# Two reservation rules in a build-time scheduler: large buffers by urgency, buffers for forms of x in order of need

## The chip, the core and the metric

The kernel runs on one core of a Trainium2 chip, float32 throughout. The metric is the device time of one execution in microseconds; the kernel before takes 1688.47 us (median of 4 runs, 1687.31 to 1689.02). The core has five engines with a queue each, which wait for one another by semaphores: TensorE (PE in the profile; its weight loads are PEld), VectorE (DVE), ScalarE (ACT), GpSimd (POOL) and SyncE (SP), which here only issues DMAs.

## The reference

A linear attention without softmax, RMS-normalised, feeds a mixture of four two-layer networks that are all evaluated and weighted:

```
kv  = einsum("bhsd,bhse->bhde", k, v)            # b 8, h 8, s 576, d 64
o   = einsum("bhsd,bhde->bhse", q, kv)
o   = o / sqrt(mean(o*o, -1) + 1e-6) * g_norm
x   = o as (b*s, h*d)                             # 4608 x 512
p   = domain_probs / (sum(domain_probs, -1) + 1e-9)
out = sum over e of p[:, e] * (relu(x @ w1[e]) @ w2[e])   # e 4, w1 512x1024, w2 1024x512
```

## The kernel before, in words

**Tiling.** The 4608 rows are cut into nine chunks of 512: for each of the eight batches its first 512 rows, and one chunk made of the eight remainders of 64 rows. The outer loop runs over the four experts, the inner one over the nine chunks; a pass `s = 9*e + c` is one chunk against one expert. The attention of batch c+1 is worked in among the passes of expert 0, so that x of a chunk is made one pass ahead.

**Fewer products, more sums.** The matrix products of a pass are done by a Strassen-Winograd scheme, for most of them in two levels: seven products of sums and differences of blocks instead of eight. The first pass of all, `up_plain` (line 1050), uses plain products. The others need forms, which are sums of blocks: of w1 and w2 (once for each expert), of x (once for each chunk), of the hidden layer (in each pass). The sums are `combine` (line 375) on VectorE or GpSimd; products go through `halves_of` (line 352; its matmul is L356 in the profile), in `up` (line 946) and in `down` and `down_deep` (1173, 1221).

**Forms of x.** `x_forms(c, key)` (line 854) makes forms 5, 6, 7 and 4 of chunk c, each in a buffer of the kind `xf`; the others lie in the chunk's own halves and in small buffers. After its inner sums each form is copied to DRAM by `keep` (line 894, a DMA of SyncE, L898). Experts 1 to 3 load all seven from there: `x_again` (line 908, issued by `load`, L385), into buffers of the kind `xf` too. There are five of them. Chunk 0 is a special case: pass 0 is plain, so its forms are made for the copies alone.

**Buffers.** The kind `big` is 31 buffers of 128 x 1024 (line 311), later two more. It holds halves of x, weights and their forms, hidden blocks, products and accumulators. A buffer is given to a tile when the operation that first writes it is placed in the order, and returned after its last use.

**The planner.** No order is written by hand. Every operation is entered by `add` (line 59) with a key (its place in the passes: 8.6 is six tenths into pass 8), its engine and a price. `layout` (line 84) plays the program through once, at build time, with these prices, and so fixes the order on each engine and the buffer of each tile; the kernel then issues the operations in that order. For each engine that is free, it looks at the waiting operations within a reach of the first one's key (line 49, `REACH`), and takes:

- for TensorE and SyncE the first that is ready, in the order of keys,
- for the others the ready one with the smallest due time.

A due time is the TensorE work that lies before the operation's key, plus 30 us of allowance if it isn't TensorE's own (`LATE`, line 53), and never later than what its consumers need. `ready` (line 122) decides whether an operation can start: its inputs' writers have been placed, and enough buffers of each kind that it has to open are in the list of free ones (which counts those that will come free at a known time). SyncE's loads must leave some over unless their key is nearly reached:

```python
    SPARE = {"big": 6, "small": 3, "xf": 3}
    FORMS = 9.0
                spare = self.SPARE.get(k, 0) if k != "xf" or op.key < self.FORMS else 0
```

While TensorE has nothing to do before key 0, `layout` fills in transposes into spare banks (`idle`, line 1438, L1440).

**Weights.** Those of expert e+1 come in during the last pass of expert e and the first of the next: `weights_1` and `weights_2` (lines 450, 510), by SyncE into `big`, and for some forms by a ScalarE copy and an accumulating DMA of GpSimd (`subtract_from`, line 436).

Of the kernel before, what the change touches and what calls it, by code (L numbers as in the profile page):

```python
# [35 lines left out]
class Plan:  # L36
# [15 lines left out]
    FORMS = 9.0  # L52
    STEP, LATE = 44.0, 30.0
    SLOW = 6.8

    def __init__(self):
        self.ops = []
# [26 lines left out]
    def layout(self, slots, later, idle, idle_banks, idle_until):  # L84


        free = {k: [(0.0, i) for i in range(len(v))] for k, v in slots.items()}
        slots = {k: list(v) for k, v in slots.items()}
        later = list(later)
        live = {}  # L90
        for b in {b for op in self.ops for b in op.bufs}:
            live[b.kind] = live.get(b.kind, 0) + 1
        ended = {}
        todo = {e: [] for e in self.REACH}
        for n, op in enumerate(self.ops):
            op.n = n
            for e in op.cost:
                todo[e].append(op)
        for e in todo:
            todo[e].sort(key=lambda o: (o.key, o.n))  # L100
        keys, begun, spent = [], [], 0.0
        for op in todo["PE"]:
            keys.append(op.key)
            begun.append(spent)
            spent += op.cost["PE"]
        begun.append(spent)
        for op in self.ops:
            at = begun[bisect.bisect_left(keys, op.key)]
            op.due = at + (0.0 if "PE" in op.cost else self.LATE)
        for op in reversed(self.ops):  # L110
            for d in op.deps:
                cross = self.SAME if op.cost.keys() == d.cost.keys() else self.CROSS
                d.due = min(d.due, op.due - cross - min(d.cost.values()))
        busy = {e: 0.0 for e in todo}
        bus, port = 3.8, 0.0
        lanes = [0.0] * self.LANES
        t = 0.0
        wake = [0.0, 1.6]
        left = len(self.ops)
        order = []  # L120

        def ready(op, eng):
            when = 0.0
            for d in op.deps:
                if d.start is None:
                    return None
            for d in op.deps:
                when = max(when, d.end + (self.SAME if d.eng == eng else self.CROSS))
            need = {}
            for b in op.outs:  # L130
                if b.kind is not None and b.slot is None:
                    need[b.kind] = need.get(b.kind, 0) + 1
            for k, n in need.items():
                spare = self.SPARE.get(k, 0) if k != "xf" or op.key < self.FORMS else 0
                if len(free[k]) < n + (spare if eng == "SP" and op.key > front + 0.1 else 0):
                    return None
                when = max(when, sorted(free[k])[n - 1][0])
            if eng == "SP":
                when = max(when, lanes[0])
            if op.port:  # L140
                when = max(when, port)
            return when

        while left:
            moved = False
            while todo["PE"] and todo["PE"][0].start is not None:
                todo["PE"].pop(0)
            front = todo["PE"][0].key if todo["PE"] else 1e9
            for eng in todo:
                if busy[eng] > t:  # L150
                    continue
                pending = todo[eng]
                while pending and pending[0].start is not None:
                    pending.pop(0)
                if not pending:
                    continue
                reach = pending[0].key + self.REACH[eng]
                best = None
                for op in pending:
                    if op.key > reach:  # L160
                        break
                    if op.start is not None:
                        continue
                    if best is not None and op.due >= best.due:
                        continue
                    when = ready(op, eng)
                    if when is None:
                        continue
                    if when > t:
                        heapq.heappush(wake, when)  # L170
                        continue
                    best = op
                    if eng in ("PE", "SP"):
                        break
                if best is not None:
                    op = best
                    op.start, op.eng = t, eng
                    if eng == "SP":
                        busy[eng] = t + op.cost[eng]
                        bus = max(bus, t + 1.5) + op.kb / 215.0  # L180
                        op.end = bus + 0.5
                        lanes = lanes[1:] + [op.end]
                    else:
                        op.end = busy[eng] = t + op.cost[eng]
                        if op.kb:
                            op.end += 9.0 if op.kb == 512 else 8.0
                    if op.port:
                        port = op.end
                        heapq.heappush(wake, port)
                    for b in op.outs:  # L190
                        if b.kind is not None and b.slot is None:
                            free[b.kind].sort()
                            b.slot = free[b.kind].pop(0)[1]
                            b.ap = slots[b.kind][b.slot]
                    for b in op.bufs:
                        b.left -= 1
                        if b.left == 0 and b.kind is not None:
                            end = max(o.end for o in [op] + b.readers + b.writers) + self.CROSS
                            free[b.kind].append((end, b.slot))
                            live[b.kind] -= 1  # L200
                            ended[b.kind] = max(end, ended.get(b.kind, 0.0))
                            for rule in [r for r in later if not any(live.get(k) for k in r[0])]:
                                later.remove(rule)
                                end = max(ended[k] for k in rule[0])
                                for ap in rule[2]:
                                    free.setdefault(rule[1], []).append((end, len(slots[rule[1]])))
                                    slots[rule[1]].append(ap)
                                heapq.heappush(wake, end)
                    heapq.heappush(wake, busy[eng])
                    heapq.heappush(wake, op.end + self.SAME)  # L210
                    heapq.heappush(wake, op.end + self.CROSS)
                    order.append(op)
                    left -= 1
                    moved = True
                if eng == "PE" and busy[eng] <= t and 1.6 <= t and front < idle_until:
                    kind, spare = next((
                        (k, f) for k in idle_banks for f in free[k] if f[0] <= t
                    ), (None, None))
                    if spare is not None:
                        took = 0.43 if t < self.SLOW else 0.23  # L220
                        op = Op(front, {"PE": took}, None, (), (), 0, False)
                        op.start, op.eng, op.end = t, eng, t + took
                        op.fn = lambda eng, bank=slots[kind][spare[1]]: idle(bank)
                        busy[eng] = op.end
                        free[kind].remove(spare)
                        free[kind].append((op.end, spare[1]))
                        heapq.heappush(wake, op.end)
                        order.append(op)
                        moved = True
            if moved:  # L230
                continue
            while wake and wake[0] <= t:
                heapq.heappop(wake)
            assert wake, ("no operation can start", t, left, {
                e: (todo[e][0].key, todo[e][0].fn) for e in todo if todo[e]
            }, {k: len(v) for k, v in free.items()})
            t = heapq.heappop(wake)
        self.length = max(o.end for o in order)
        return order
# [1251 lines left out]
```

## Time and profile before

| | |
|---|---|
| median of 4 runs | 1688.47 us (1687.31 to 1689.02) |
| the profiled execution, its own time | 1688.64 us |
| its span, first to last instruction | 1686.5 us |
| TensorE matmul busy, and weight loads | 1676.9 us (99%), 1571.7 us (93%) |
| VectorE, ScalarE, GpSimd busy | 1240.4, 978.2, 715.2 us (74%, 58%, 42%) |
| DMA traffic | 234.27 MB, mean 139 GB/s |
| granted TensorE clock | 1.000 |

A line of the profile names a line of the kernel, an engine, an operation, and written tiles before read ones by kind (`xf<-big`); a count after x, then times. `SPq` is SyncE's queue: what it shows is the issue of a DMA. L379 is every sum made by `combine`, so its groups are told apart by tiles. A table of waits gives the sum in us, how often, and the longest. A line of a stretch gives its length, then the busy time of PE, PEld, DVE, ACT and POOL with their instructions, the granted clock, the DMA share and GB/s. The chain of waits is followed back from the last instruction, each step to what released it.

### The profile page before, as it was taken

How to read it: one execution, taken by the hardware profiler on the slowest of the kernel's cores; microseconds unless marked ns; L12 is line 12 of the kernel's file. 1: busy time of each engine (PE TensorE's matmuls, PEld its weight loads, DVE VectorE, ACT ScalarE, POOL GpSimd, SP SyncE). 2: the span in 40 equal slices, each digit the busy share in tenths (PEclk: the TensorE clock that was granted, in tenths of full speed). 3: DMA queues.
4: the chain of work that ended last, by engine and by line, in shares of the span. 5: the costliest groups of instructions: out<-in, count | busy, mean ns of one | idle time of the engine just before them, and what ended most of it. 6: DMA issues, size and time to landing. Idle time of an engine off the chain costs nothing.

```text
span 1686.5 us, 66495 instructions
## 1 busy us (share of the span) xinstructions
PE 1676.9 (99%) x29038; PEld 1571.7 (93%) x29038; DVE 1240.4 (74%) x2045; ACT 978.2 (58%) x2405; POOL 715.2 (42%) x672
## 2 busy tenths in 40 slices
PE   9999999999999999999999999999999999999998
PEld 6687888888889999999999999999999999999996
DVE  4865665575787788777787887877787886877774
ACT  3454555455555666666666666666666666666662
POOL 3613433333454344344455445444446446444431
PEclk9999999999999999999999999999999999999999
DMA  9855453642556344444568444444478444444442
GB/s 240 252 182 157 161 156 105 203 140 96 199 160 163 115 114 114 114 114 110 132 179 200 115 114 114 115 115 113 111 189 201 121 114 115 115 114 114 115 102 51
DMA packets 172330, 234.27 MB, mean 139 GB/s; under 512 B 61576, under 2 KB 112648, under 8 KB 172040
## 3 DMA queue, kind: packets, MB, share of 16 engines
q1 hardware_dynamic: 148968, 193.32, 36.2%
q0 software_dynamic: 23072, 36.71, 14.9%
q8 instruction: 228, 3.74, 0.9%
q14 instruction: 62, 0.51, 0.1%
HBM read 155.79 MB, written 74.19 MB: 136 GB/s over the span
## 4 chain that ended last, share of the span: by engine, by line
PE 99%; DMA 0%; issue 0%; ACT 0%; POOL 0%; DVE 0%; POOLq 0%
PE u L356 47%; PE db L356 32%; PE ab L356 14%; PE ab L716 1%; PE ab L761 1%; PE ab L693 1%; PE ab L743 1%; PE ab L1440 1%; DMA xf<-x 0%; PE ab L805 0%; PE ab L697 0%; PE db L743 0%; PE ab L787 0%; PE ab L821 0%; PE u L743 0%
## 5 line engine op out<-in xcount | busy, mean ns | idle before, releaser
L379 DVE TENSOR_TENSOR big<-big,big 128x1024 f32<-128x1024 f32 (+1 forms) x517 | 501.9, 985 | 43.2 <-ACT big L959 16.7
L356 PE MATMUL u<-xf,big 128*64 128x128 f32 x7072 | 504.8, 273 | 0.8 <-DMA xf<-x 0.8
L356 PEld LDWEIGHTS u<-xf,big 128*64 128x64 f32 x7072 | 409.5, 137 | 5.2 <-DMA xf<-x 1.0
L356 PE MATMUL u<-xf,w1y 128*64 128x128 f32 x5304 | 382.8, 273 | 0.0
L356 PE MATMUL db<-big,big 128*64 128x128 f32 (+1 forms) x4328 | 362.1, 307 | 0.0
L1003 DVE TENSOR_TENSOR big<-u,snap 128x256 f32<-128x256 f32 x464 | 194.5, 422 | 213.3 <-PE u L356 147.4
L356 PEld LDWEIGHTS u<-xf,w1y 128*64 128x64 f32 x5304 | 307.7, 137 | 4.3 <-issue 1.3
L356 PEld LDWEIGHTS db<-big,big 128*64 128x64 f32 x4328 | 264.4, 137 | 39.3 <-issue 0.5
L995 ACT ACTIVATE snap<-u 128x256 f32<-128x256 f32 x490 | 188.0, 384 | 193.7 <-PE u L356 138.7
L379 POOL TENSOR_TENSOR big<-big,big 128x256 f32<-128x256 f32 (+1 forms) x156 | 191.1, 1228 | 167.3 <-DVE big L379 75.0
L995 ACT ACTIVATE big<-u 128x256 f32<-128x256 f32 x464 | 177.6, 385 | 89.2 <-PE u L356 69.0
L379 POOL TENSOR_TENSOR big<-big 128x512 f32<-128x512 f32 (+1 forms) x76 | 95.5, 1257 | 161.1 <-DVE big L379 104.8
L1304 ACT ACTIVATE snap<-db 128x256 f32<-128x256 f32 (+1 forms) x230 | 82.6, 359 | 114.2 <-PE db L356 101.7
L959 ACT ACTIVATE big<-big 128x1024 f32<-128x1024 f32 x133 | 139.9, 1052 | 4.4 <-DVE big L379 4.0
L1312 DVE TENSOR_TENSOR big<-ab,snap 128x256 f32<-128x256 f32 x164 | 69.2, 422 | 58.4 <-PE ab L356 28.5
L1161 POOL DMA_DIRECT2D out_dram<-big x98 | 88.4, 1025 | 55.8 <-ACT big L1138 43.5
L1342 POOL TENSOR_TENSOR big<-big 128x512 f32<-128x512 f32 x34 | 44.1, 1297 | 154.0 <-DVE big L379 140.7
L995 ACT ACTIVATE u<-u 128x256 f32<-128x256 f32 x245 | 91.0, 372 | 28.5 <-PE u L356 14.3
L379 DVE TENSOR_TENSOR big<-big 128x512 f32<-128x512 f32 (+1 forms) x121 | 103.4, 858 | 0.4 <-ACT big L1138 0.2
L356 PE MATMUL ab<-big,big 128*64 128x128 f32 (+1 forms) x1352 | 94.7, 276 | 0.1
L356 PE MATMUL db<-small,big 128*64 128x128 f32 x1240 | 90.6, 273 | 0.0
L356 PE MATMUL ab<-kv,big 128*64 128x128 f32 x1200 | 83.2, 273 | 0.0
(178 smaller groups left out, 2415.4 us busy)
## 6 DMA issues: line engine op xcount, KB each, us to landing
xf<-x SPq DMA_DIRECT2D x108, 512.0 KB, 3.6
out_dram<-big POOLq DMA_DIRECT2D x82, 256.0 KB, 5.6
xf<-x_h SPq DMA_DIRECT2D x81, 256.0 KB, 3.1
xf<-x SPq DMA_DIRECT2D x81, 256.0 KB, 3.7
x<-xf SPq DMA_DIRECT2D x36, 512.0 KB, 4.9
big<-in_moe_w_dram SPq DMA_DIRECT2D x31, 512.0 KB, 5.8
x_h<-big SPq DMA_DIRECT2D x18, 512.0 KB, 3.3
big<-in_moe_w_dram POOLq DMA_DIRECT2D x17, 512.0 KB, 6.2
```

Of the source, the lines that this page charges most:

```text
L356: nc.tensor.matmul(out_[cols], lhsT=lhsT[:, cols], rhs=rhs, **kw)
L379: lambda eng: adder(eng).tensor_tensor(out=out_(), in0=a(), in1=b(), op=op),
L693: nc.tensor.transpose(bank.ap[:, rs], qt.ap[:, rs], ident[:])
L716: nc.tensor.matmul(bank.ap[r * D:(r + 1) * D, o * D:(o + 1) * D], lhsT=ks[r], rhs=vs[r], start=(j == 0), stop=(j == len(sets) - 1), skip_g ...
L743: nc.tensor.matmul(raw[r].ap[c * D:(c + 1) * D, (o * NR + i) * D:(o * NR + i + 1) * D], lhsT=qTs[hp].ap[half, at:at + D], rhs=kv.ap[half, ...
L959: lambda eng: nc.scalar.activation(out=b.ap[:], in_=b.ap[:], func=ACT.Relu),
L995: lambda eng: nc.scalar.activation(out=where(), in_=ps.ap[:, 0:HN], func=ACT.Copy),
L1003: lambda eng: nc.vector.tensor_tensor(out=block(whole, a, t), in0=src.ap[:, 0:HN], in1=add_.ap[:], op=ALU.add),
L1161: nc.gpsimd.dma_start(out=dst, in_=cell(i)[parts, :], accum_op=ALU.add)
L1304: lambda eng: nc.scalar.activation(out=where(), in_=group_of(ps.ap), func=ACT.Copy),
L1312: lambda eng: nc.vector.tensor_tensor(out=cell(tq, dq), in0=group_of(src.ap), in1=group_of(add_.ap), op=ALU.add,),
L1342: lambda eng: adder(eng).tensor_tensor(out=whole(to), in0=whole(a), in1=whole(b), op=ALU.add),
```

## The change

Three constants name the kinds concerned and a tolerance, and two rules are added to `ready`.

**Large buffers.** `waiting["big"]` holds each operation, other than a SyncE load, whose inputs have all been placed and which still has to open a large buffer, with the planned end of its last input. An operation that wants a large buffer may take one only if the free ones exceed its own need by the number of waiting operations that have an earlier due time and whose inputs end within 0.3 us from now. SyncE's loads have no claim of their own, but are held to the rule.

**Forms of x.** `first["xf"]` holds each operation that opens a buffer of the kind `xf` and has not been placed. No operation may open such a buffer while another one there has an earlier due time. This holds for `x_forms` and `x_again` alike.

Prices, due times, keys, numbers of buffers and the operations themselves stay.

```diff
@@ -52,6 +52,7 @@
     FORMS = 9.0
     STEP, LATE = 44.0, 30.0
     SLOW = 6.8
+    SHARED, AHEAD, INORDER = ("big",), 0.3, ("xf",)
@@ -111,6 +112,34 @@
             for d in op.deps:
                 cross = self.SAME if op.cost.keys() == d.cost.keys() else self.CROSS
                 d.due = min(d.due, op.due - cross - min(d.cost.values()))
+        missing, after = {}, {op: [] for op in self.ops}
+        for op in self.ops:
+            missing[op] = len(op.deps)
+            for d in op.deps:
+                after[d].append(op)
+        waiting = {k: {} for k in self.SHARED}
+
+        def arm(op):
+            for b in op.outs:
+                if b.kind in waiting and b.slot is None and "SP" not in op.cost:
+                    waiting[b.kind][op] = max([d.end for d in op.deps] or [0.0])
+
+        for op in self.ops:
+            if not missing[op]:
+                arm(op)
+        first, known = {k: {} for k in self.INORDER}, set()
+        for op in self.ops:
+            for b in op.outs:
+                if b.kind in first and b not in known:
+                    known.add(b)
+                    first[b.kind][op] = True
+
+        def claimed(kind, op):
+            return sum(
+                1 for o, since in waiting[kind].items()
+                if o.due < op.due and since <= t + self.AHEAD and o is not op
+            )
+
@@ -133,6 +162,10 @@
                 if len(free[k]) < n + (spare if eng == "SP" and op.key > front + 0.1 else 0):
                     return None
+                if k in waiting and len(free[k]) < n + claimed(k, op):
+                    return None
+                if k in first and any(o.due < op.due for o in first[k] if o is not op):
+                    return None
                 when = max(when, sorted(free[k])[n - 1][0])
@@ -192,6 +225,12 @@
                             b.slot = free[b.kind].pop(0)[1]
                             b.ap = slots[b.kind][b.slot]
+                    for held in list(waiting.values()) + list(first.values()):
+                        held.pop(op, None)
+                    for o in after[op]:
+                        missing[o] -= 1
+                        if not missing[o]:
+                            arm(o)
                     for b in op.bufs:
```

## The prediction

> **What bounds the kernel now.** I read the page first, then the waits of TensorE, then the record in stretches, and last the places at which the two new rules can act. The page:
>
> ```profile
> span 1686.5 us, 66495 instructions
> PE 1676.9 (99%) x29038; PEld 1571.7 (93%) x29038; DVE 1240.4 (74%) x2045; ACT 978.2 (58%) x2405; POOL 715.2 (42%) x672
> ```
>
> TensorE is busy 99%. The modelled ends of matmuls can flatter that number, so I went to the waits of TensorE, all five of them (sum, times, longest):
>
> ```profile
> PE ab L716 <- issue: 1.9, 1, 1.9
> PE ab L1440 <- POOL ident masks.py:199: 1.4, 1, 1.4
> PE u L356 <- DMA xf<-x: 0.8, 1, 0.8
> PE ab L1440 <- issue: 0.4, 1, 0.4
> PE ab L821 <- ACT big L769: 0.3, 1, 0.3
> ```
>
> They sum to 4.8 us. The timeline puts the three of L716 and L1440, 3.7 us, before 24 us. Only 1.1 us of waiting lies later: 0.3 at 65.64 us (L821) and 0.8 at 536 us, where a form of x comes late. The record in stretches (PE, PEld, DVE, ACT, POOL busy, clock, DMA):
>
> ```profile
> 30.00:40.00 10.00, 10.00 (x100) 4.93 (x98) 7.28 (x17) 3.33 (x9) 0.12 (x1) 1.00 0.94 236
> 40.00:50.00 10.00, 10.00 (x113) 4.39 (x110) 9.85 (x14) 4.75 (x12) 5.52 (x7) 1.00 0.76 174
> 480.00:520.00 40.00, 39.98 (x685) 37.90 (x682) 31.83 (x58) 21.57 (x52) 13.88 (x16) 1.00 0.67 185
> 520.00:560.00 40.00, 39.21 (x720) 38.96 (x718) 33.50 (x64) 24.84 (x60) 17.68 (x17) 1.00 0.56 134
> 560.00:600.00 40.00, 40.00 (x736) 39.82 (x733) 30.79 (x56) 25.34 (x66) 16.22 (x12) 1.00 0.41 121
> 600.00:640.00 40.00, 40.00 (x738) 40.00 (x736) 32.21 (x54) 25.14 (x65) 17.91 (x16) 1.00 0.44 113
> ```
>
> From 600 us on both TensorE columns are full, while VectorE has about 8 of every 40 us free and ScalarE 15. So at a given amount of matmul work the time is this floor plus whatever makes TensorE wait. The change alters no instruction, only their order and their buffers, so it can take away 4.8 us at most by waits, and can add without limit.
>
> **What the Trainium skill says.** Perfetto Trace Analysis, "Identifying the Most-Contended Engine": matmul busy time is a bad metric, and the busy share of weight loads is the good one. The trace agrees: weight loads fill 40.00 of 40 us after 600 us, but only 4.39 of 10 at 40 to 50 us, where the matmuls have 512 columns. The same page, "Optimization Strategy": gaps that repeat on the engine that should be saturated can mean that buffers ran out. No such gap is in TensorE's waits, so a scarce buffer does not stop it now. DMA: Bandwidth & Descriptors, "Anatomy of one DMA — SWDGE (gpsimd) path": DMA engines do not wait on semaphores, the issuing sequencer does. SyncE's own waits agree: a load that waits for a buffer holds all loads behind it.
>
> ```profile
> SPq L385 <- PE u L356: 938.8, 208, 9.0
> ```
>
> **The change, part by part.**
>
> (1) Forms of x are placed by due time. The keys that sort them come from lines of the planner that the change leaves alone; they are keys, not chip times. For forms 5, 6, 4, 7 of chunk 0 they are 71.1, 71.9, 72.6 and 85.6; for chunk 1 they are 59.2, 59.9, 60.7 and 85.8. Chunk 0's forms serve only the copies kept in DRAM, so the rule puts them behind 5, 6 and 4 of chunk 1, and form 7 of chunk 1 behind all four of them. Today three of chunk 0's run early, the first at 39 us; chunk 1's stand at 68.26 (POOL), 72.23, 73.57 and 90.31 us:
>
> ```profile
> 39.05 0.68 DVE L379 TENSOR_TENSOR xf<-big 128x512 f32<-128x512 f32 x1
> 73.57 0.69 DVE L379 TENSOR_TENSOR xf<-big,xf 128x512 f32<-128x512 f32 x1
> 90.31 0.68 DVE L379 TENSOR_TENSOR xf<-big,big 128x512 f32<-128x512 f32 x1
> 103.58 0.61 PE L356 MATMUL u<-xf,big 128*64 128x128 f32 x8
> ```
>
> Each moved form is one operation of 0.68 us, one of 0.42 and two of 0.28: 1.66 us; three make 5.0 us of VectorE work that leaves 39 to 60 us. TensorE waits there for nothing, so I count the relief as 0, with 0.3 (L821) as its best. At the new place VectorE has the room (10.9 of 20 us at 80 to 100).
>
> The five buffers decide what is late next. Chunk 1 holds three until TensorE has read them, so chunk 0's four go through two in two turns. A turn is 1.66 of work, some 0.6 to issue the copy, and 4.9 to land (the page's median for x<-xf): 7.2 us. Form 7 of chunk 1 starts at 74.2 + 2 x 7.2 = 88.6 and is ready at 90.3; TensorE reads it at 103.58. That leaves 13 us of cover, cost 0. Their copies move too: on SyncE, two at 62.79 and one or two later wait for the new work, and the q, k and v loads of chunk 2 and 3 stand behind them. Those loads feed attention a pass later, and SyncE has a gap of 8.6 us there (95.1 to 103.7), so 0. The two large buffers of chunk 0 are given back some 13 to 17 us later; that is part of (3).
>
> (2) The first forms of expert 1. Today's written order loads form 1 of chunk 1 (due 503.6) and form 3 of chunk 0 (494.1) before form 1 of chunk 0 (469.5), because only keys under 9 must leave three buffers. A buffer is thus parked for 60 us, and later loads come when TensorE has no reserve left. The chain at that place:
>
> ```profile
> 528.34 1.33 PE u L356 x24
> 529.67 0.02 issue
> 529.69 6.39 DMA xf<-x
> 536.08 0.04 issue
> 536.12 1.09 PE u L356 x16
> ```
>
> With the rule these two stand behind, all five buffers turn over, and the wait goes: -0.8 us. If another load takes its place, 0.
>
> (3) Large buffers are kept. In the written order of before, 1031 large buffers are given out; in 685 cases three or fewer of the pool were left, so the rule acts everywhere, not at one place. It moves buffers from operations with time to those without. As TensorE waits for no such operation, there is no gain to have. The cost is bounded from below by 0, and from above by loads that come too late: weights. The last quarter of w1 of expert 1 is issued at 467.47 and lands about 5.8 us later. POOL forms two sums at 473.54 and 476.36 (2.4 each), and the inner sums end near 487.3. The x form used with it is issued at 498.33 and lands 3.6 later, at 501.9. So the weights have about 15 us of cover, VectorE its 8 of 40 us. I take 0.
>
> Before 24 us and after the last matmul (1681.8, then 4.7 us of drain) nothing changes: at first at least 15 large buffers are free and no form of x is made; at the end six or more are free.
>
> **Sum.** -0.8 (2), 0 for (1) and (3), -0.1 as a third of the 0.3 at L821. Profiled execution: 1686.5 - 0.9 = 1685.6 span, with the 2.1 around it 1687.7 against its own 1688.64. The median of the runs is 0.17 lower than that execution, so I forecast 1687.6, a change of -0.05%. No difference below 0.2%, 3.4 us, can be told from none.
>
> **The rivals.** *Inert* (0.10): another load is as late, 1688.5. For it: loads of forms wait for TensorE 208 times anyway. *Likeliest* (0.58): 1687.6, own range 1685.3 to 1690.
>
> *Weights too late* (0.20, slower): an operation with an earlier due time claims each buffer that comes free; the loads of the next expert also must leave six, and their due time counts 0.55 us for an issue that needs 5.8 to land. At 15 us of delay the cover is used up; each us beyond stops TensorE at each of three expert changes. From 15 + (3.4 + 0.8) / 3 = 16.4 us it is slower by more than 0.2%. At 18 us it is 9 us: 1696.6; at 20 us 1703. Against it: a load's urgency rises with time, and claims fall away once served.
>
> *Form 7 late* (0.07, slower): if VectorE's queue or SyncE doubles each turn, form 7 comes at 74.2 + 28.8 + 1.7 = 104.7, only 1 us late; only tripled turns, 119.1 us, lose 15 less what TensorE can take in between, about 8: 1695.
>
> *Faster* (0.05): TensorE's small attention pieces cost a pause at each change of shape; its weight loads show some 19 us of such pauses at the attention lines, 0.2 to 0.3 each. If the new order put 14 more of them side by side: 14 x 0.3 = 4.2, 1684.2. Nothing in the rules aims at that.
>
> **How the numbers follow.** Same: 0.58 + 0.10 = 0.68. Slower: 0.20 + 0.07 = 0.27. Faster: 0.05. The low end 1685.2 is the bound of faster; the high end 1697.5 takes in half of the late weights (0.10) and most of form 7 (0.05): 0.83 inside.
>
> **What would show it.** Right: first form of chunk 0 after 70 us instead of 39; loads at 447 to 535 us in order of need; no wait of TensorE for xf at 536; its waits after 25 us at or under 1 us; weight loads later by less than 15 us. Wrong: waits of TensorE for big or xf at 440 to 540, 870 to 930 or 1280 to 1330 us; gaps on TensorE between 60 and 110; or a different TensorE pace with no waits, which would mean that the order of shapes moved the time.

## The result, and the profile after

The changed kernel takes 1686.1 us (median of 42 runs, 1684.49 to 1690.85) against 1688.03 us (63 runs): a ratio of 0.9988, 95% interval 0.9984 to 0.9993. In a second series it was 0.9984 (0.9978 to 0.9991), 1685.96 against 1688.13. So it is faster by 1.9 to 2.2 us, 0.12 to 0.16%. The prediction said 1687.6, within 0.2% of before, with a gain of 0.9 us at the end of its sum.

The page of the changed kernel, its span and busy times:

```profile
span 1684.3 us, 66427 instructions
PE 1675.2 (99%) x29038; PEld 1571.5 (93%) x29038; DVE 1218.0 (72%) x2050; ACT 980.7 (58%) x2405; POOL 703.6 (42%) x667
```

The same 29038 matmuls, 2.2 us less span. Five sums have moved from GpSimd to VectorE (672 to 667, 2045 to 2050): the planner also chooses the engine of a sum. Code lines stand 39 further down in this kernel: L395 is the product that was L356, L424 the load that was L385. All waits of TensorE:

```profile
PE ab L755 <- issue: 1.8, 1, 1.8
PE ab L1479 <- POOL ident masks.py:199: 1.4, 1, 1.4
PE ab L860 <- ACT big L808: 0.3, 1, 0.3
PE ab L1479 <- issue: 0.2, 1, 0.2
PE ab L755 <- DMA big<-in_v_dram: 0.2, 1, 0.2
```

The wait for a form of x is gone; 0.3 us is left after the first 25 us (L860, the old L821). The stretches around the change of expert, in the columns of the prediction:

```profile
480.00:520.00 40.00, 40.00 (x690) 38.20 (x686) 33.33 (x61) 23.83 (x54) 17.97 (x21) 1.00 0.61 176
520.00:560.00 40.00, 40.00 (x738) 40.00 (x734) 32.02 (x59) 24.73 (x61) 18.58 (x17) 1.00 0.61 140
560.00:600.00 40.00, 40.00 (x738) 40.00 (x736) 33.16 (x57) 26.02 (x68) 17.99 (x16) 1.00 0.43 122
```

The count in brackets after TensorE's busy time is the one to read. A stretch full of the short products holds 738 matmuls, 54 ns each. Before, the three held 685, 720 and 736; now 690, 738 and 738. That is 25 matmuls, 1.4 us, though the two busy times of the first stretch differ by only 0.02 us.

Stretches by the clock shift against one another from kernel to kernel, so for the comparison I take the time from the start of one matmul in the trace to that of another, by their place among the 29038 (the count is the same in all kernels):

| stage, by matmul | before | after | difference |
|---|---|---|---|
| start: first to 500th | 42.23 us | 41.90 us | -0.33 |
| attention and expert 0: to the 7001st | 412.59 | 412.17 | -0.42 |
| last pass of expert 0: to the 7501st | 35.72 | 35.82 | +0.10 |
| change to expert 1: to the 9501st | 110.70 | 109.17 | -1.53 |
| experts 1 to 3: to the 28501st | 1037.73 | 1037.68 | -0.05 |
| last product and drain | 46.18 | 46.22 | +0.04 |

The start differs from one execution to the next by more than the whole effect: over the 13 profiles of this study it takes 40.5 to 45.7 us, and 41.9 and 43.0 in the two profiles of the changed kernel, so its -0.33 means nothing. The stages behind it repeat: the second profile of the changed kernel gave 412.17, 35.82, 109.17 and 1037.69 again. The order of before was profiled twice too (the second time as rules_off, below): 412.59 and 412.59, but 110.70 and 110.97 at the change of expert, where its wait for a form of x took 0.8 us once and 1.1 the other time. So a difference of 0.1 us in the attention stage can be read, and at the change of expert the gain is 1.5 to 1.8 us.

### The profile page after: what moved, and what is told of

Read it like the earlier page. It is cut to its first block, busy times and chain, and to the rows that moved or that the text cites. A ratio compares the mean times of both kernels' runs of the same rounds, so it can differ in the third digit from the quotient of the medians.

```text
span 1684.3 us, 66427 instructions
## 1 busy us (share of the span) xinstructions
PE 1675.2 (99%) x29038; PEld 1571.5 (93%) x29038; DVE 1218.0 (72%) x2050; ACT 980.7 (58%) x2405; POOL 703.6 (42%) x667
## 4 chain that ended last, share of the span: by engine, by line
PE 99%; DMA 1%; issue 0%; ACT 0%; SPq 0%; DVE 0%; ACTq 0%
PE u L395 47%; PE db L395 32%; PE ab L395 14%; PE ab L755 1%; PE ab L800 1%; PE ab L732 1%; PE ab L782 1%; DMA big<-in_v_dram 1%; PE ab L844 0%; PE ab L826 0%; PE db L782 0%; PE ab L860 0%; PE ab L1479 0%; SPq L424 0%; PE ab L736 0%
## 5 line engine op out<-in xcount | busy, mean ns | idle before, releaser
L418 DVE TENSOR_TENSOR big<-big,big 128x1024 f32<-128x1024 f32 (+1 forms) x525 | 509.4, 986 | 51.4 <-ACT big L998 21.3
L395 PE MATMUL u<-xf,big 128*64 128x128 f32 x6784 | 486.5, 273 | 0.2
L395 PEld LDWEIGHTS u<-xf,big 128*64 128x64 f32 x6784 | 392.8, 137 | 5.7 <-issue 1.3
L395 PE MATMUL u<-xf,w1y 128*64 128x128 f32 x5304 | 386.7, 273 | 0.0
L1042 DVE TENSOR_TENSOR big<-u,snap 128x256 f32<-128x256 f32 x478 | 200.9, 422 | 250.2 <-PE u L395 153.3
L395 PE MATMUL db<-big,big 128*64 128x128 f32 (+1 forms) x4304 | 362.2, 307 | 0.0
L418 POOL TENSOR_TENSOR big<-big,big 128x256 f32<-128x256 f32 (+1 forms) x204 | 236.2, 1170 | 261.0 <-DVE big L418 124.1
L395 PEld LDWEIGHTS u<-xf,w1y 128*64 128x64 f32 x5304 | 308.9, 137 | 3.0 <-issue 0.5
L395 PEld LDWEIGHTS db<-big,big 128*64 128x64 f32 x4304 | 263.4, 137 | 39.3 <-issue 0.3
L1034 ACT ACTIVATE big<-u 128x256 f32<-128x256 f32 x478 | 182.9, 385 | 80.3 <-PE u L395 57.2
L1343 ACT ACTIVATE snap<-db 128x256 f32<-128x256 f32 (+1 forms) x230 | 82.5, 358 | 110.8 <-PE db L395 103.5
L395 PE MATMUL db<-small,big 128*64 128x128 f32 x1512 | 113.8, 274 | 0.0
L1200 POOL DMA_DIRECT2D out_dram<-big x106 | 94.1, 1028 | 34.5 <-ACT big L1177 29.6
L1381 POOL TENSOR_TENSOR big<-big 128x512 f32<-128x512 f32 x19 | 24.8, 1306 | 166.2 <-DVE big L418 134.2
L395 PE MATMUL ab<-big,big 128*64 128x128 f32 (+1 forms) x1328 | 93.4, 276 | 0.0
L1177 ACT ACTIVATE big<-big,p_all 128x256 f32<-128x256 f32 x186 | 88.2, 501 | 4.1 <-POOL big L1381 3.7
```

Source lines behind the costliest of these rows:

```text
L395: nc.tensor.matmul(out_[cols], lhsT=lhsT[:, cols], rhs=rhs, **kw)
L418: lambda eng: adder(eng).tensor_tensor(out=out_(), in0=a(), in1=b(), op=op),
L1034: lambda eng: nc.scalar.activation(out=where(), in_=ps.ap[:, 0:HN], func=ACT.Copy),
L1042: lambda eng: nc.vector.tensor_tensor(out=block(whole, a, t), in0=src.ap[:, 0:HN], in1=add_.ap[:], op=ALU.add),
L1177: lambda eng: nc.scalar.activation(out=cell(i, half), in_=ap(), func=ACT.Copy, scale=prob()),
L1200: nc.gpsimd.dma_start(out=dst, in_=cell(i)[parts, :], accum_op=ALU.add)
```

## The experiments

Three theories were set against each other. **Expert change:** the gain is the wait at 536 us, and what else stops TensorE between 490 and 600. **Shapes:** the new order has fewer changes between small attention pieces and products on TensorE, each of which costs a pause. **Large buffers:** their rule pays by itself, in expert 0 too. The rule for large buffers with no rule for forms of x has no run: with it the planner comes to a point in pass 8 at which no operation can start, so there is no such order.

### One rule at a time

```diff
# xf_loads: changed kernel, only this part of the rules
-    SHARED, AHEAD, INORDER = ("big",), 0.3, ("xf",)
+    SHARED, AHEAD, INORDER = (), 0.3, ("xf",)
-                if k in first and any(
+                if k in first and eng == "SP" and any(
# xf_sums: the same with   eng != "SP"
# xf_only: the first edit alone
# big_xfloads: the second edit alone
```

> Kernel before, with the in-order rule for forms of x held only against SyncE's loads (experts 1 to 3 and the change to them); the order up to about 430 us is that of before. Parked-buffer theory (the gain is the wait of TensorE for a form of x at 536 us): no wait for xf between 500 and 560, 1.0 to 1.4 us faster than before, half or more of the change's gain. Theory of shapes (the gain comes from fewer pauses at small attention pieces before 420 us): 0, within 0.3 us. Theory of large buffers (their rule makes the gain): 0, within 0.3 us.

> Kernel before, with the in-order rule held only against the sums on VectorE and GpSimd that make forms of x during expert 0. Parked-buffer theory: the wait for a form of x at about 536 us stays, 0.5 to 1.2 us; time as before within 0.5 us. Theory of shapes: up to 0.5 us faster, seen on TensorE between 80 and 420 us. The prediction's part (1): no wait of TensorE added between 60 and 110 us, form 7 of chunk 1 in time.

> Both halves of the in-order rule for forms of x, no rule for large buffers. Parked-buffer theory: as the loads alone, 1.0 to 1.6 us faster than before, no wait for xf at 500 to 560. Theory of large buffers: a third or less of the change's gain of 1.9 us, under 0.7 us.

> The changed kernel without the in-order rule for the sums: large buffers by urgency, and SyncE's loads of forms in order. Parked-buffer theory: 1.0 to 1.6 us faster than before, the same as with the loads alone within 0.5 us. Theory of large buffers: 0.5 us or more faster than the loads alone, with less waiting on TensorE somewhere. Rival of late weights: waits of TensorE for big at 440 to 540, 870 to 930 or 1280 to 1330 us; the prediction expects none.

| kernel | median (before: 1687.98) | ratio, 95% | change to expert 1 | attention stage |
|---|---|---|---|---|
| before | | | 110.70 us (110.97) | 412.59 us |
| xf_loads | 1687.37 | 0.9998 (0.9990 to 1.0006) | 110.03 | 412.59 |
| xf_sums | 1687.89 | 1.0003 (0.9995 to 1.0011) | 110.97 | 411.89 |
| xf_only | 1687.96 | 0.9999 (0.9991 to 1.0007) | 110.31 | 411.89 |
| big_xfloads | 1686.41 | 0.9991 (0.9983 to 1.0000) | 109.17 | 412.77 |

The times cannot tell the first three from before, so the 1.0 us or more that was expected of xf_loads and xf_only did not come. The trace shows how much did at the expert change in the profiled execution: 0.67 and 0.39 us, a few tenths more against the second profile of before. With the loads in order the wait for xf is gone, but another has taken part of its place. TensorE's waits of xf_loads, all but those of the first 25 us:

```profile
PE db L395 <- ACT snap L1343: 0.5, 1, 0.5
PE ab L860 <- ACT big L808: 0.3, 1, 0.3
```

And its three stretches:

```profile
480.00:520.00 40.00, 39.52 (x678) 37.55 (x676) 31.03 (x55) 22.28 (x52) 18.88 (x18) 1.00 0.67 179
520.00:560.00 40.00, 40.00 (x738) 40.00 (x736) 33.94 (x62) 23.35 (x60) 20.25 (x17) 1.00 0.56 136
560.00:600.00 40.00, 40.00 (x734) 39.82 (x732) 29.86 (x55) 25.90 (x67) 17.25 (x14) 1.00 0.38 114
```

The 18 matmuls missing at 520 to 560 are back, while 480 to 520 lacks 12 now, where before lacked 5. The rule for large buffers removes that remainder: 110.03 to 109.17, with the same loads. What is lost here can be read one level below TensorE's own list, in the waits of its weight loads. Between 485 and 600 us, first those of before, then those of xf_loads:

```profile
PEld u L356 <- DMA xf<-x: 1.0, 1, 1.0
PEld db L356 <- ACT ab L1304: 0.3, 1, 0.3
PEld db L356 <- ACT big L1304: 0.2, 1, 0.2
```

```profile
PEld db L395 <- ACT snap L1343: 0.7, 1, 0.7
PEld db L395 <- ACT big L1343: 0.2, 1, 0.2
```

The first list adds up to 1.5 us, which is what the full change gains in this stage; the second to 0.9, which is what the rule for large buffers gains on top of the loads. big_xfloads and the changed kernel have no wait of a weight load in this stretch. All waits but that for xf are for ScalarE (L1304, in the later text L1343), which copies a product out of one of the two `db` banks. In the timeline of before, the weight load of the 0.3 starts at 511.96 us, right after ScalarE's copy of a product that TensorE had only just finished (511.54 to 511.91), with eight matmuls of another product in between; in xf_loads no other product lies between. My reading is that this time is lost where TensorE's order comes back to `db` too soon; the records do not name the bank. How a rule for buffers changes that order was not traced. Nor can it be read from VectorE: before has one wait of 2.3 us there for an output copy that still held a large buffer, but it lasts from 512.6 to 515.0 us, after the 0.3 had passed and 78 us ahead of the 0.2. xf_loads has one as long, over at 513.1 us, a microsecond before its 0.7 begins.

In xf_sums, too, the expected wait for xf did not stay: 1.4 us of waiting for ScalarE's snapshot (L1343) stood in its place, and the stage took 110.97 us. In both kernels whose loads are not held in order, TensorE is stopped there by one thing or another.

big_xfloads against xf_loads is the pair that decides: the theory of the parked buffer alone expected the same time within 0.5 us, that of large buffers a lead of 0.5 or more; the medians differ by 0.96 and the stage by 0.86. The intervals of the two overlap; it is the stage that decides: against 110.03 here, 109.17 came back in six profiles, those of the changed kernel (twice), big_xfloads and, below, big_late, late_02 and pack.

The attention stage has an effect of its own. With the sums held in order it is 0.70 us shorter than before (xf_sums, xf_only), and 0.60 shorter when the rule for large buffers is there too (412.77 to 412.17). The rule for large buffers makes it 0.2 to 0.3 longer. The full change is left with -0.42.

### The rule for large buffers at the expert change only

```diff
# big_late: on top of big_xfloads
-                if k in waiting and len(free[k]) < n + claimed(k, op):
+                if k in waiting and front >= 8.0 and len(free[k]) < n + claimed(k, op):
```

> Kernel before, with SyncE's loads of forms in order and the rule for large buffers only once TensorE's front has reached pass 8 (about 430 us); up to there the order is that of before. Theory of the expert change (both rules pay between 490 and 600 us and nowhere else): TensorE takes 109.2 us there, as with the change, against 110.7 before; 1.2 to 1.9 us faster than before in the span. Theory that the rule for large buffers pays in expert 0 too: 0.5 us or more of the change's gain missing.

1686.15 us against 1688.24, ratio 0.9989 (0.9981 to 0.9997): the time of the full change within the noise. The change of expert takes 109.17 us, the same as with the full change, and the attention stage 412.48, 0.3 more than with it. The stretches:

```profile
480.00:520.00 40.00, 40.00 (x690) 38.27 (x688) 31.28 (x62) 23.69 (x55) 21.20 (x20) 1.00 0.71 185
520.00:560.00 40.00, 40.00 (x737) 40.00 (x735) 31.54 (x62) 23.99 (x62) 16.97 (x18) 1.00 0.55 128
560.00:600.00 40.00, 40.00 (x738) 40.00 (x736) 30.55 (x53) 24.59 (x65) 18.11 (x15) 1.00 0.42 126
```

So the eight passes before it, in which both rules also act with the full change, contribute 0.3 us in the trace, too little for the times to show. The theory of the expert change holds for most of the gain, 1.53 us of about 2. Of these the loads in order give 0.67, and the rule for large buffers on top of them 0.86.

### Later weights

```diff
# late_02: on top of the changed kernel, in ready()
+            if need.get("big") and eng == "SP" and op.kb == 512 and not op.deps and op.key > 7.9:
+                if op.key > front - 0.2:
+                    return None
# late_04: the same with 0.4
```

> The changed kernel; SyncE's loads of the weights of experts 1 to 3 are held until TensorE's front is 0.2 of a pass beyond their key (before and after: from 0.1 ahead of it), so they come roughly 5 to 13 us later. The prediction's cover of 15 us: TensorE loses under 1 us at each expert change, within 0.2% of the changed kernel. Rival of late weights with no cover: 3 to 10 us at each change, 1695 to 1715.

> As the run before, held until 0.4 of a pass beyond the key, roughly 9 us later than there and up to 22 us later than in the changed kernel. Cover of 15 us: about 2 to 7 us lost at each of three changes, 1692 to 1707, seen as waits of TensorE near 500, 930 and 1330 us. If nothing is lost the cover was larger than predicted; if much more, smaller.

late_02: 1687.2 against 1688.24, ratio 0.9993 (0.9985 to 1.0001). In the trace it loses nothing: 109.17 us at the first change, 1037.35 for the passes that follow. That is its fastest execution, 1685.03 us; the median is 1.1 to 1.2 us behind that of the changed kernel, so others may lose a little. late_04: 1700.48 us, ratio 1.0069 (1.0056 to 1.0083). The two longest waits of TensorE (L398 is the product here):

```profile
PE u L398 <- DVE big L1045: 6.1, 2, 3.3
PE u L398 <- ACT snap L1037: 2.5, 2, 1.6
```

The stretches around the second change of expert:

```profile
880.00:920.00 40.00, 39.13 (x718) 38.89 (x716) 32.47 (x56) 26.91 (x64) 21.54 (x23) 1.00 0.79 192
920.00:960.00 40.00, 37.25 (x682) 36.99 (x680) 34.56 (x67) 22.85 (x59) 24.48 (x24) 1.00 0.71 147
```

76 matmuls are missing here, 4.1 us, and TensorE waits again at 1307 and 1323 us, at the third change; at the first it loses 0.16 us in all. Delays against the changed kernel, from the issue of each load in the traces: at the second change, late_02 has at most 14.7 us (w2) and 7.6 (w1) and loses nothing; late_04 has 9.2 to 21.3 us and loses, in the profiled execution, 10.7 us after the 9501st matmul, 5.3 at each of the two changes on average, within the 2 to 7 expected. This execution, 1696.19 us, is the fastest of four; by the median late_04 is 14 us behind the changed kernel, 7 at each of the two changes if it is lost there too. At the first change late_04 delays w2 by 11 to 24 us and the last quarter of w1 by 11.8, at no loss, which was not expected. The rival of late weights exists, then. In the profiled executions its cover at the second and third change ends between 15 and 21 us of delay if w2 sets it, between 8 and 21 if w1 does; the prediction worked out 15, for w1 at the first change, where the 11.8 did no harm. The changed kernel doesn't use it up: its own last quarter of w1 is issued at 464.71 us, 2.8 us earlier than before, and the largest shift that it brings, the third load of w2 at the second and third change, is 10 us (889.49 to 899.85, and 1274.86 to 1285.32).

### Four buffers for forms of x

```diff
-        "big": (31, 2 * NT), "w1y": (7, 768), "xf": (5, 2 * NT), "snap": (5, HN),
+        "big": (31, 2 * NT), "w1y": (7, 768), "xf": (4, 2 * NT), "snap": (5, HN),
```

> The changed kernel with four buffers for forms of x instead of five. The prediction's part (2) held that the wait at 536 us came from one of five buffers being parked for 60 us; this parks one for good, with the order kept. If a missing buffer is what costs: TensorE waits for xf again, 0.5 us or more between 490 and 600, and it may at each of the later passes (24 of them, up to 0.3 us each, 7 us in all). If the order of the loads is what counts: 109.2 us there as with the change, no wait for xf after 600, within 1 us of the changed kernel.

1688.85 against 1688.13, ratio 1.0004 (0.9995 to 1.0013): 2.9 us behind the changed kernel on the same chip. Neither expectation is met. TensorE waits for no form of x, as the order theory says, yet the change of expert takes 110.58 us and the passes after it 1.4 us more than with the change. What it waits for, besides the start and L860:

```profile
PE u L395 <- DVE big L1042: 0.7, 1, 0.7
PE u L395 <- ACT big L1034: 0.5, 1, 0.5
```

Both (at 870 and 587 us) are waits for work on large tiles. So one buffer less for forms of x does cost, 1.4 us at the change of expert, about what the change gains there, but it does not show as a wait for xf: TensorE stops for other tiles. How the shortage gets from one kind to the other was not traced. And a buffer taken away for good is more than one parked for 60 us.

### The rules switched off, and the change again

```diff
# rules_off
-    SHARED, AHEAD, INORDER = ("big",), 0.3, ("xf",)
+    SHARED, AHEAD, INORDER = (), 0.3, ()
```

> The text of the changed kernel with both rules switched off, so that the order and the buffers are those of before instruction by instruction. All theories: the span of before, 1685.8 us in the median, the wait for a form of x at 536 us there, TensorE 110.7 us between 490 and 602. What is open: the changed kernel and every variant of it so far spend 1.8 to 1.9 us around the span, before 2.1. If 1.8 here too, 0.3 us of the measured gain of 1.9 comes with the program's text and not from the rules; if 2.1, with the order.

> The changed kernel unaltered, on the chip of the two runs above, to set them against: 1.6 us less span than before in the median, 1.8 us around the span.

rules_off: 1688.29 against 1688.13, ratio 0.9998 (0.9990 to 1.0006); median span 1686.1 us, as before; the wait for xf is there again, and the change of expert takes 110.97 us, the attention stage 412.59. Its profiled execution is long (1692.36 us) because the first 500 matmuls took 45.7 us:

```profile
PE u L395 <- DMA xf<-x: 1.1, 1, 1.1
```

Around the span it spends 2.11 us, as before (2.10), where the changed kernel spends 1.79. So 0.3 us of the difference lie outside the first and last instruction and come with the order, not with the text. after_again has a median span of 1684.2 us, 1.9 less than before in that series; 1.9 and 0.3 are its 2.2. The stages behind the start, -0.42 and -1.53 with the small ones, add up to 1.9 as well.

### Fewer changes of shape

```diff
# pack: on top of the changed kernel, in TensorE's choice (bookkeeping left out);
# op.small is a piece that is no L356 product
+                    if eng == "PE" and best is not None:
+                        if op.key > best.key + 0.2:
+                            break
+                        if op.small:
+                            best = op
+                            break
+                        continue
+                    if eng == "PE" and op.small and not small and op.key > front + 0.2:
+                        held.append(op)
+                        if len(held) < 2:
+                            continue
+                        best = held[0]
+                        break
                     best = op
-                    if eng in ("PE", "SP"):
+                    if eng == "SP" or (eng == "PE" and (op.small or not small)):
                         break
+                if best is None and held:
+                    best = held[0]
...
                     op.start, op.eng = t, eng
+                    if eng == "PE":
+                        small = op.small
```

> The changed kernel, with one more rule for TensorE: after a small attention piece it takes another one if one is ready within 0.2 of a pass, and a single one far ahead of the front is held until a second is ready. Changes between small pieces and products in TensorE's order fall from 161 to 147 (before: 167). Theory of shapes (each change costs 0.1 to 0.15 us): 1.4 to 2.1 us faster than the changed kernel, between 80 and 420 us. If the pauses do not depend on neighbours: 0.

1684.89 us, ratio to before 0.9980 (0.9972 to 0.9987): ahead of both kernels in the median, by 3.3 and by 1.1 to 1.2 us, though its interval overlaps that of the change, so the second lead is likely and not settled. In the trace the attention stage takes 411.49 us, 0.68 less than with the change, where 1.4 to 2.1 was expected. One wait at 65.7 us is longer; it takes the place of the 0.3 us at L860 (L414 is the product in this kernel):

```profile
PE u L414 <- ACT u L1053: 0.6, 1, 0.6
```

Without the 0.3 us more it would have been 0.9 us for 14 changes of shape: 0.05 to 0.07 us each, where the prediction put 0.3. That supports the theory of shapes as a mechanism, by one order. It does not explain the change itself: before has 167 changes of shape, xf_sums 165, big_xfloads 163 and the changed kernel 161, and their attention stages take 412.59, 411.89, 412.77 and 412.17 us. That the order of the sums moves this stage is measured; how it does so was not found.

## Why the prediction was right

**The class and the floor: right in the main.** Where TensorE is full its pace did not change: experts 1 to 3 past the first change keep theirs within 0.05 us. Faster by 0.12% is within the 0.2% band at 0.68, and the range holds it. Two statements were too strong: that no difference below 0.2% can be told from none (with 42 and 63 runs this one was), and that the floor plus TensorE's list of waits is the whole time.

**Part (2), the forms of expert 1: right that the wait goes, near in its size.** Forecast -0.8 us for loads in order; xf_loads measured -0.67 (110.70 to 110.03; -0.94 against the second profile of before). 0.5 us came back as a wait on ScalarE. That the parked buffer made the wait is not settled: xf_sums does not hold the loads in order, and its wait for xf went too.

**Part (3), large buffers: the step that failed.** It said "As TensorE waits for no such operation, there is no gain to have", after "a scarce buffer does not stop it now". The same loads with and without the rule take 109.17 and 110.03 us: -0.86 where 0 stood. The list of TensorE's waits leaves small pauses out. Its own table of stretches had a sign: at 560 to 600 us TensorE is busy 40.00, but with 736 matmuls and 39.82 us of weight loads, where the full stretch after it has 738 and 40.00. (A low share of weight loads is a sign only between stretches of like shapes: the 4.39 of 10 us at 40 to 50 us goes with 512-column matmuls, and TensorE is busy for all 10 there.) The waits of the weight loads name 0.5 us there besides that for xf. Its other half held: no loss by late weights, and a cover that the delayed loads don't contradict.

**Part (1), the forms of expert 0: no loss, as it said, but by a smaller margin than worked out, and the relief was not 0.** That "TensorE waits there for nothing" hid a gain here too: the sums in order take 0.6 to 0.7 us off the attention stage. The free time of VectorE at the new place is 9.1 us of 20; the 10.9 is what it was busy. Sums and products of this stage in the changed kernel:

```profile
76.31 0.68 DVE L418 TENSOR_TENSOR xf<-big 128x512 f32<-128x512 f32 x1
89.80 0.69 DVE L418 TENSOR_TENSOR xf<-big,xf 128x512 f32<-128x512 f32 x1 [1.64 <-PE u L395]
97.39 0.68 DVE L418 TENSOR_TENSOR xf<-big,big 128x512 f32<-128x512 f32 x1
102.01 0.61 PE L395 MATMUL u<-xf,big 128*64 128x128 f32 x8
```

Chunk 0's forms moved from 39 us to 76, behind those of chunk 1. The first turn of a buffer took 13.5 us (76.31 to 89.80), not 7.2. Form 7 of chunk 1 started at 97.39, where the sum said 88.6, its last inner sum ended at 100.35, and TensorE read an xf form next at 102.01: some 1.7 us of cover instead of 13. The term that was mis-sized is the turn, priced by its own work and landing, with nothing for the queues of VectorE and SyncE. The rival "form 7 late" was closer than its 0.07 suggests; that nothing was lost was in part luck.

**The 0.1 us at L821:** not realised, the wait of 0.3 us stands.

**The sum.** Forecast -0.9. Measured in the two profiles: -1.53 at the expert change, -0.42 in the attention stage, -0.33 at the start, +0.09 elsewhere, -2.2 in all; 0.3 more lies around the span. The start is chance. So the gain is about twice the forecast: 0.7 of the 1.5 us at the expert change and the 0.4 of the attention stage stood at 0 in it, because no wait of TensorE's list was there.

## What to carry to other kernels

When one engine is saturated, read its lost time from how much work each stretch holds and from the waits of its weight loads, not from its list of waits alone: here 0.7 of a gain of 1.5 us was in pauses too short for that list. When a wait is removed, look at what stands in its place: the loads in order took away 0.8 us and 0.5 came back. And when a change in a scheduler is claimed to act everywhere, restrict it to one stretch: here pass 8 onwards gave nearly all of it. Compare stages by the same matmuls and profile one order twice: that showed which stage is chance (the start) and which repeats to 0.01 us.

## What was not expected of the hardware

The time around the span belongs to the order of a program: 2.1 us for before and for the same order under the new text, 1.8 to 1.9 for nine other orders, that of the change among them, and 2.0 for pack. What of an order sets it was not found. The first 500 matmuls take 40.5 to 45.7 us from one execution to the next, more than anything the change moves, while the 6500 after them take 412.59 us in three profiles of one order and 412.17 in four of another.
